# Attention, Fourier mixing and routed experts on one core: logits moved forward in the group, attention banks merged, readers of banks ahead, longer pauses

## The chip, the core and the metric

The kernel runs on one core of a Trainium2 chip. The metric is the device time of one execution in microseconds, the median of three runs. The core's engines work side by side, each through a queue of its own: TensorE (PE) multiplies matrices, VectorE (DVE), ScalarE (ACT) and GpSimd (POOL) work on elements, and the sync engine (SP) issues nearly all DMA transfers. TensorE writes its results to PSUM, eight banks of 2 KB in each of 128 partitions (512 numbers of 32 bits); another engine reads a bank before TensorE may fill it anew.

## What is computed

Three parts follow each other for 8 batches of 576 tokens of width 512: an attention through 32 packed queries, a mixing with a Fourier transform and a two-layer network, and a layer of eight experts of which each token takes one.

```python
p_packed = sm_attn(p, k, v)                 # 8 heads, p: 32 x 64, k and v: 576 x 64
out = sm_attn(q, p_packed, p_packed)
...
X = np.fft.fft(np.fft.fft(x, axis=1), axis=2)
u = x + np.real(X)
un = (u - mu) / np.sqrt(var + 1e-06)
x = u + np.maximum(un @ w_ch1, 0.0) @ w_ch2
...
logits = np.einsum('bsd,de->bse', x, w_gate)
local_gate = sigmoid(x @ w_local)           # under 0.5: the best expert of this token; else that of the token before
h = np.maximum(x[b, s] @ w1[e], 0.0)
out[b, s] = p[e] * (h @ w2[e])              # p: softmax of the logits
```

## The kernel before

Most products run on numbers split into two 16-bit parts, high and low, in three passes (PASS). First attention(0) runs alone (the first 81.5 us of the profile). Then come ten groups: b0, b1, b2, R0, b3, b4, b5, b6, R1, b7. A group bN is the channel mix of batch N (class Mix): 16 steps mm1(f) of 12 matmuls 512 columns wide into a bank hp, and 16 steps mm2(f) of 12 such matmuls into four banks acc, mm2 two steps behind mm1 (LEAD), 384 matmuls in all. ScalarE and VectorE make ht from hp between the two. R0 and R1 are the same for rows left over from four batches, half as wide. In the profile's rows the mix of b4 has the names hp18 and acc18 to acc21. Behind the groups the expert stage runs, from 1045.6 us.

Beside the mix of batch N runs, as a generator, attention(N + 1): at each tick of the mix (32 a group) it goes on by ATT_RATE yields. So a yield with nothing in front of it is a pause, and the attention's instructions stand between those of the mix, in an order that a scheduler then settles by priority when the program is built; high_priority(offset) lets an instruction pass others by that much (SOON 200, URGENT 100). In the order of a group the steps of the attention are:

- scores: s1 from k and the packed queries p, in two halves; greatest and exps read the banks; turn makes ehl and transposes it by DMA to et. The load of v is issued behind the scores, since it takes k's buffer.
- pps: et times v (vhl, two parts of v); ppr, ptp and pth are the packed result, scaled, transposed and split. The load of q is issued when v has been split, since it takes v's buffer; qh is q split by ScalarE and GpSimd.
- scores2, greatest2, exps2, sums2, divide2: s2 from q and pth, three tiles of 128, 128 and 99 rows; m2 and ee are read from its bank.
- channels: gp, the packed result times cosines and sines (cdt), four tiles of 257 columns (two halves, cosines and sines); g is gp split. fold2 and parts2 make eo, ah (transposed by DMA) and eh.
- bp (eh times cst), zd, then for three row tiles t: P and Q (cosine and sine part of the transform), qs a copy of Q, ul and uu (rl and ru for the leftover rows) sums and differences of P and qs, X (the attention's output itself), which is added to them. norm makes unh, transposed by DMA to ut, the input of the next group's mix.

After the mix of a batch, after_mix(tiles) runs as another generator at LAST_RATE yields a tick, beside the next group's mix: for each of the four tiles it scales u to xh, transposes it by DMA to xt (one buffer), stores it to XS, and multiplies it with the gate weights: lp, eight small matmuls, read by lsum. Expert weights are converted all the while (se, so, WS).

The eight PSUM banks are four for acc (psO), two for hp (psM), and two (psA) for all tiles of the attention and the logits: s1, pps, ptp, s2, gp, bp, zd, P, Q, X, lp.

## Time and profile before

| | before |
|---|---|
| median of 3 runs | 1516.62 us (1511.03 to 1521.59) |
| the profiled execution | 1514.66 us, span 1512.9 us from first to last instruction |
| TensorE busy | 1403.3 us, 93% of the span |
| VectorE, ScalarE, GpSimd busy | 769.0, 460.5, 278.9 us |
| mean granted clock of TensorE | 0.971 of full speed |

Busy time is a mean over stages of different kinds: it is to be read group by group, and where an engine stands idle the waits say which instruction of which other engine ended that. Granted clock is the share of full speed that the chip lets TensorE have; it has two levels, 1.2 and 2.4 GHz, and the value of a stretch is a mean of the two.

### The profile page before, as it was taken

The page shows a single profiled execution, that of the slowest core. Times are in us where ns is not written, and L with a number is a line of the kernel's source. Part 1 is how long each engine was busy: PE and PEld are TensorE (multiplying, and loading weights), DVE is VectorE, ACT ScalarE, POOL GpSimd, SP SyncE. Part 2 cuts the span into 40 slices and gives each one's busy share as a digit, 9 for nine tenths or more (in the row PEclk, how much of TensorE's full clock was granted, in tenths as well). Part 3 has the DMA queues.
Part 4 walks back from the last instruction along what each step waited for, and adds up shares of the span by engine and source line. Part 5 has one row for each costly group of instructions (what it writes and reads, how often), then busy time and mean ns, then how long its engine had stood idle before and what let it go on. Part 6 is the DMA issues. An engine that isn't in the chain of part 4 may idle for free. (4 is left out here: it accounts for less than half of the span.)

```text
span 1512.9 us, 28826 instructions
## 1 busy us (share of the span) xinstructions
PE 1403.3 (93%) x11340; PEld 825.5 (55%) x11340; DVE 769.0 (51%) x1615; ACT 460.5 (30%) x858; POOL 278.9 (18%) x296
## 2 busy tenths in 40 slices
PE   4588888998999899999999999999899999999996
PEld 3334434544564454454444456455677677777764
DVE  5789977567655766666766665433531111111110
ACT  3343444344333434434435333111111111111111
POOL 1312113203200420320321220000212121121211
PEclk6689999999999999999999999999999999999998
DMA  8275476386476637647656546244946636783371
GB/s 268 61 226 177 142 190 156 111 208 164 122 166 158 191 108 201 170 118 219 149 131 198 125 124 170 56 180 139 252 114 197 170 89 172 226 245 81 79 230 54
DMA packets 233163, 239.70 MB, mean 158 GB/s; under 512 B 168191, under 2 KB 179583, under 8 KB 232384
## 3 DMA queue, kind: packets, MB, share of 16 engines
q1 hardware_dynamic: 226464, 217.62, 52.6%
q0 software_dynamic: 6560, 20.19, 4.1%
q8 instruction: 91, 1.49, 0.4%
q14 instruction: 48, 0.39, 0.1%
HBM read 267.38 MB, written 53.74 MB: 212 GB/s over the span
## 5 line engine op out<-in xcount | busy, mean ns | idle before, releaser
L759 PE MATMUL acc<-w2h,ht 128*128 128x512 f16 x1728 | 410.3, 379 | 0.8 <-DVE ul L767 0.8
L739 PE MATMUL hp<-ut,w1h 128*128 128x512 f16 x1536 | 371.3, 383 | 5.9 <-DMA ut<-unh 5.2
L739 PEld LDWEIGHTS <-w1h 128*128 128x128 f16 x1920 | 183.7, 98 | 187.8 <-issue 21.0
L759 PEld LDWEIGHTS <-ht 128*128 128x128 f16 x1728 | 165.7, 98 | 185.2 <-issue 6.6
L1107 PE MATMUL ehp<-xgt,w1b 128*128 128x128 f16 x3936 | 232.6, 219 | 3.3 <-DMA w1b<-WS 2.2
L1107 PEld LDWEIGHTS <-w1b 128*128 128x128 f16 x3936 | 225.2, 98 | 15.5 <-DMA w1b<-WS 2.6
L1115 DVE SCALAR_TENSOR_TENSOR hx<-ehp,hx 128x512 f16<-128x512 f32 x82 | 56.6, 691 | 339.3 <-ACT hx L1114 335.5
L1125 PE MATMUL eo<-w2b,hx 128*128 128x512 f16 x984 | 219.2, 379 | 0.0
L747 DVE SCALAR_TENSOR_TENSOR ht<-hp,ht 128x512 f16<-128x512 f32 (+1 forms) x160 | 101.3, 633 | 165.9 <-ACT ht L746 165.7
L1125 PEld LDWEIGHTS <-hx 128*128 128x128 f16 x984 | 94.3, 98 | 106.3
L261 ACT ACTIVATE so<-se 128x512 f16<-128x512 f32 x128 | 79.8, 628 | 194.6 <-DMA WS<-so 154.6
L746 ACT ACTIVATE ht<-hp 128x512 f16<-128x512 f32 (+1 forms) x160 | 87.2, 546 | 138.6 <-PE hp L739 133.5
L1114 ACT ACTIVATE hx<-ehp 128x512 f16<-128x512 f32 x82 | 48.9, 597 | 185.9 <-PE ehp L1107 185.9
L262 DVE SCALAR_TENSOR_TENSOR so<-se,so 128x512 f16<-128x512 f32 x128 | 98.2, 776 | 10.7 <-ACT so L261 10.7
L1133 POOL DMA_INDIRECT out<-ys,sidx x41 | 41.5, 1013 | 332.2 <-ACT ys L1132 310.8
L1132 ACT ACTIVATE ys<-eo,scl 128x512 f32<-128x512 f32 x41 | 28.2, 687 | 179.2 <-PE eo L1125 179.2
L344 POOL TENSOR_TENSOR qh<-q,qh 128x1420 f16<-128x1420 f32 x12 | 34.6, 2880 | 257.3 <-ACT qh L343 233.9
L1075 POOL DMA_INDIRECT xg<-XS,gidx x41 | 42.2, 1029 | 174.9 <-DVE sidx L1031 103.9
L368 PE MATMUL s<-k,p 64*32 64x288 f32 x256 | 24.3, 478 | 24.8 <-DVE ru L648 11.6
L739 PE MATMUL hp<-utr,w1h 128*128 128x256 f16 x384 | 47.1, 272 | 0.0
L563 PE MATMUL bp<-cst,eh 128*128 128x289 f16 (+1 forms) x192 | 33.5, 317 | 13.2 <-ACT eh L540 6.5
L694 POOL TENSOR_TENSOR unh<-un,unh 128x512 f16<-128x512 f32 x32 | 38.6, 1216 | 30.7 <-ACT unh L693 30.7
(288 smaller groups left out, 1346.4 us busy)
## 6 DMA issues: line engine op xcount, KB each, us to landing
w1b<-WS SPq DMA_DIRECT2D x156, 512.0 KB
w2b<-WS SPq DMA_DIRECT2D x156, 512.0 KB
se<-in_w SPq DMA_DIRECT2D x64, 512.0 KB
WS<-so SPq DMA_DIRECT2D x128, 256.0 KB
sw<-in_wc SPq DMA_DIRECT2D x32, 512.0 KB
q<-in_qd SPq DMA_DIRECT2D x16, 710.0 KB
v<-in_vd SPq DMA_DIRECT2D x16, 640.0 KB
k<-in_kd SPq DMA_DIRECT2D x16, 576.0 KB
```

The costliest lines, as they stand in the source:

```text
L261: nc.scalar.activation(dst_hi, src, AF.Copy, scale=scale)
L262: nc.vector.scalar_tensor_tensor(dst_lo, src, scale, dst_hi, ALU.mult, ALU.subtract)
L739: nc.tensor.matmul(hp[:, :ntok], w1h[:, f, c, x], ut[:, 4 * y + c, :ntok], start=n == 0, stop=n == 11)
L746: nc.scalar.activation(ht[:, 0, :ntok], hp[:, :ntok], AF.Relu)
L747: pace[0] = nc.vector.scalar_tensor_tensor(ht[:, 1, :ntok], hp[:, :ntok], 0.0, ht[:, 0, :ntok], ALU.max, ALU.subtract).ins
L759: nc.tensor.matmul(self.acc[j], ht[:, x, 128 * j:128 * j + 128], w2h[:, f, y], start=f == 0 and n == 0, stop=f == 15 and n == 2)
L1075: nc.gpsimd.indirect_dma_start(out=g_, out_offset=None, in_=XS[0:rows], in_offset=bass.IndirectOffsetOnAxis(ap=gidx[:, b:b + 1], axis=0), ...
L1107: nc.tensor.matmul(hp[:, cols], w1b[b % RB][:, 2 * c + fg, x, cols], xt[b][:, 4 * y + c], start=n == 0, stop=n == 11, skip_group_check=True)
L1114: nc.scalar.activation(ht[:, fg, 0], hp, AF.Relu)
L1115: nc.vector.scalar_tensor_tensor(ht[:, fg, 1], hp, 0.0, ht[:, fg, 0], ALU.max, ALU.subtract)
L1125: nc.tensor.matmul(op, h[:, f // 4, x, 128 * (f % 4):128 * (f % 4) + 128], w2b[b % RB][:, f, y], start=n == 0, stop=n == 23)
L1133: nc.gpsimd.indirect_dma_start(out=A["out"], out_offset=bass.IndirectOffsetOnAxis(ap=sidx[:, b:b + 1], axis=0), in_=ys, in_offset=None, bo ...
```

## The change

Logits: LAST_RATE goes from 1.2 to 3, so that after_mix is done in the first third of the next group. Banks: cosines and sines share a gp tile of 512 columns (two of the sine's columns are always zero and are left out), so channels is called twice instead of four times; Q stands behind P in one bank for t < 2, and 24 small memsets on GpSimd set the two missing columns of qs to zero. Readers: the ScalarE and VectorE operations that read a bank of psA get an offset of 100 (freeing). Scores: only seven of the eight matmuls of a half get the offset of 200, so that they follow the first, which stands where the program has it. Pauses: one more yield ahead of pps (twice), behind pth and in each of the row tiles t, three more behind channels; ATT_RATE goes from 2.3 to 2.6. fold2 makes eo ahead of ah.

```diff
-    cd = np.concatenate([np.cos(2 * np.pi * ((c * k2) % 512) / 512), np.sin(2 * np.pi * ((c * k2) % 512) / 512)], 1)
+    cd = np.concatenate([np.cos(2 * np.pi * ((c * k2) % 512) / 512),
+                         np.sin(2 * np.pi * ((c * k2[:, 1:256]) % 512) / 512)], 1)
...
-ATT_RATE = 2.3
+ATT_RATE = 2.6
...
-LAST_RATE = 1.2
+LAST_RATE = 3
...
+    def freeing():
+
+        return tc.high_priority(offset=URGENT)
...
+            for n in range(8):
+                i, p2, r = n // 4, n // 2 % 2, n % 2
+                d, row = slice(64 * r, 64 * r + 64), 64 * p2 + 32 * r
+                with tc.high_priority(offset=SOON if n else 0):
+                    nc.tensor.matmul(s1[hf][i][row:row + 32, :288], pt[d, 2 * hf + p2],
+                                     kts[hf][d, p2, 288 * i:288 * i + 288], start=True, stop=True)
...
-                with tc.high_priority(offset=SOON if fn in (scores, greatest, exps) else 0):
+                with tc.high_priority(offset=SOON if fn in (greatest, exps) else 0):
...
+            yield
             n = 0
             for t in range(5):
...
-        nc.scalar.copy(pth[:, 0], ptp[:, :256])
-        nc.vector.tensor_tensor(pth[:, 1], ptp[:, :256], pth[:, 0], op=ALU.subtract)
+        with freeing():
+            nc.scalar.copy(pth[:, 0], ptp[:, :256])
+            nc.vector.tensor_tensor(pth[:, 1], ptp[:, :256], pth[:, 0], op=ALU.subtract)
...
-        yield
-        yield
+        for _ in range(3):
+            yield
...
-        g = ap.tile([128, 2, 2, 2, 257], F16, tag="g", name=f"g{b}")
...
+        g = ap.tile([128, 2, 2, 512], F16, tag="g", name=f"g{b}")
+
+        def channels(hf):
+            gp = att(f"gp{b}_{hf}")
             for n, (x, y) in enumerate(PASS):
                 for p2 in range(2):
...
+                    nc.tensor.matmul(gp[64 * p2:64 * p2 + 64],
                                      pth[:, x, 128 * hf + 64 * p2:128 * hf + 64 * p2 + 64],
...
+                                     cdt[:, 2 * hf + p2, y], start=n == 0, stop=n == 2, skip_group_check=True)
+            with freeing():
+                nc.scalar.copy(g[:, hf, 0], gp)
+                nc.vector.scalar_tensor_tensor(g[:, hf, 1], gp, 1.0, g[:, hf, 0], ALU.mult, ALU.subtract)
...
-            nc.vector.tensor_reduce(m2[:, 0], s3, axis=AX.X, op=ALU.max)
...
+            with freeing():
+                nc.vector.tensor_reduce(m2[:, 0], s3, axis=AX.X, op=ALU.max)
+                nc.vector.tensor_tensor(efs[i].rearrange("p (g j) -> p g j", j=32), s3,
+                                        m2[:, 0].unsqueeze(2).to_broadcast([nr, 16, 32]), op=ALU.subtract)
...
-                      ((channels, 1), (parts2, 1), (divide2, 2)), ((fold2, 2),), ((channels, 2), (parts2, 2)), (),
-                      ((channels, 3),), ()):
+                      ((parts2, 1), (divide2, 2)), ((fold2, 2),), ((channels, 1), (parts2, 2)), (), (), (), (), ()):
...
             P = att(f"P{b}_{t}")
-            Q = att(f"Q{b}_{t}") if t < 2 else P
+            Q = P[RQ, 257:512] if t < 2 else P[RQ, 1:256]
+            qs = qs0 if t == 0 else ap.tile([128, 576], F32, tag="f32w", name=f"qs{b}_{t}", bufs=4)
+            nc.gpsimd.memset(qs[R, 0:257:256], 0.0)
...
-                nc.tensor.matmul(Q[RQ, :257], bt[:, hf, x, 1, s0:s0 + M], g[:, hf, y, 1], start=n == 0, stop=n == 5,
+                nc.tensor.matmul(Q, bt[:, hf, x, 1, s0:s0 + M], g[:, hf, y, 257:], start=t == 2 and n == 0, stop=n == 5,
...
+            with freeing():
+                nc.scalar.copy(qs[R, 1:256], Q)
...
+            with freeing():
+                nc.vector.tensor_tensor(ul[R, :256], P[R, :256], qs[R, :256], op=ALU.subtract)
+                nc.vector.tensor_tensor(uu[R, :256], P[R, :256], qs[R, :256], op=ALU.add)
...
+            with freeing():
+                nc.vector.tensor_reduce(lsum, lp[:, :18].rearrange("p (y e) -> p e y", y=2), axis=AX.X, op=ALU.add)
```

Left out are the same wrappings around the operations that read bp, zd, X and the second half of P.

The built program shows what this moves. First TensorE in b4's group (names as above; lp12 to lp15 are the logits of b3's four tiles, and 5 is the attention of batch 5), before:

```order
L427 MATMUL pps5_6004<-vhl5_0_6005,et5_0_5949 64x128
...
L776 MATMUL lp12_6132<-wgh_110,xt12_5975 128x18
...
L442 MATMUL ptp5_6177<-ident_78,ppr5_6161 128x128 x2
...
L491 MATMUL s2_5_0_6215<-pth5_6194,qh5_0_6086 128x64
...
L776 MATMUL lp13_6301<-wgh_110,xt13_6158 128x18
...
L491 MATMUL s2_5_2_6313<-pth5_6194,qh5_0_6086 128x64
...
L469 MATMUL gp5_0_6370<-cdt_94,pth5_6194 64x257
...
L469 MATMUL gp5_1_6420<-cdt_94,pth5_6194 64x257
...
L469 MATMUL gp5_2_6464<-cdt_94,pth5_6194 64x257
...
L469 MATMUL gp5_3_6489<-cdt_94,pth5_6194 64x257
...
L776 MATMUL lp14_6510<-wgh_110,xt14_6367 128x18
...
L563 MATMUL bp5_0_0_6529<-cst_92,eh5_0_6400 128x289
```

And TensorE in the same group, after:

```order
L373 MATMUL s1_5_0_0_5801<-k5_0_5797,p5_5794 32x288 x2
...
L373 MATMUL s1_5_1_0_5845<-k5_1_5799,p5_5794 32x288 x2
...
L793 MATMUL lp12_5897<-wgh_110,xt12_5825 128x18
...
L793 MATMUL lp13_5964<-wgh_110,xt13_5918 128x18
...
L433 MATMUL pps5_5928<-vhl5_0_5929,et5_0_5874 64x128
...
L793 MATMUL lp14_6054<-wgh_110,xt14_6017 128x18
...
L793 MATMUL lp15_6146<-wgh_110,xt15_6073 128x18
...
L497 MATMUL s2_5_0_6189<-pth5_6158,qh5_0_6039 128x64
...
L497 MATMUL s2_5_2_6261<-pth5_6158,qh5_0_6039 128x64
...
L476 MATMUL gp5_0_6319<-cdt_94,pth5_6158 64x512
...
L476 MATMUL gp5_1_6394<-cdt_94,pth5_6158 64x512
...
L569 MATMUL bp5_0_0_6444<-cst_92,eh5_0_6346 128x289
```

Counted in matmuls of the mix from the group's start, the scores s1_5 stood 24 and 13 ahead of the start, at the end of b3's group, and stand at 54 and 65 now; pps at 96 and 117, now 97 and 120; the logits at 120, 171, 219 and 279, now 80, 97, 117 and 141; the last s2 at 171, now 168; the four gp at 180, 189, 201 and 210, now two at 180 and 198; the first bp at 222, now 225. P and Q of t = 0 stood at 249 and the second X behind them at 270, both unchanged. Groups b2, b3, b5 and b6 look alike, but in b3 the scores stood at 36 to 56 before already, with pps at 84 and s2 at 141.

The sync engine's queue in the same stretch, before (v, q and k are loads from memory, WS1, WS2 and XS stores, se loads of expert weights):

```order
L329 DMA v5_0_5892<-in_vd 128x5x256
L329 DMA v5_1_5937<-in_vd 128x5x256
L391 DMA_TRANSPOSE et5_0_5949<-ehl5_0_5945 128x10x128
...
L334 DMA q5_0_6015<-in_qd 128x1420
L391 DMA_TRANSPOSE et5_1_5982<-ehl5_1_5978 128x10x128
...
L334 DMA q5_1_6078<-in_qd 128x1420
L798 DMA_TRANSPOSE xt12_5975<-xh12_5942 128x8x128
L799 DMA XS_124<-xh12_5942 128x1024
...
L798 DMA_TRANSPOSE xt13_6158<-xh13_6058 128x8x128
```

And the sync engine's queue there, after:

```order
L334 DMA v5_0_5811<-in_vd 128x5x256
L816 DMA_TRANSPOSE xt12_5825<-xh12_5816 128x8x128
...
L334 DMA v5_1_5855<-in_vd 128x5x256
...
L396 DMA_TRANSPOSE et5_0_5874<-ehl5_0_5870 128x10x128
L816 DMA_TRANSPOSE xt13_5918<-xh13_5867 128x8x128
...
L396 DMA_TRANSPOSE et5_1_5913<-ehl5_1_5909 128x10x128
L339 DMA q5_0_5949<-in_qd 128x1420
...
L816 DMA_TRANSPOSE xt14_6017<-xh14_5954 128x8x128
...
L339 DMA q5_1_6028<-in_qd 128x1420
L816 DMA_TRANSPOSE xt15_6073<-xh15_6036 128x8x128
```

The loads of q5 were issued 9 and 38 matmuls into the group and are issued at 97 and 112 now; v5 and the transposes et5, ahead of or at the group's start before, now stand among four transposes for logits (xt12 at 65, xt13 at 85, xt14 at 104, xt15 at 120).

VectorE around the last s2 of that group, before (m2 and ee read its bank, g reads gp's):

```order
L498 TENSOR_REDUCE m2_5_2_6354<-s2_5_2_6313 99x16
L526 SCALAR_TENSOR_TENSOR ah5_0_6379<-ee5_0_6280,ah5_0_6379 128x512
L500 TENSOR_TENSOR ee5_2_6356<-s2_5_2_6313,m2_5_2_6354 99x512
L530 SCALAR_TENSOR_TENSOR eo5_0_6383<-ee5_0_6280 128x256
L518 TENSOR_TENSOR ee5_1_6292<-ee5_1_6292,m2_5_1_6290 128x512
L747 SCALAR_TENSOR_TENSOR ht18_7_6364<-hp18_7_6297,ht18_7_6364 128x512
L474 SCALAR_TENSOR_TENSOR g5_6214<-gp5_0_6370,g5_6214 128x257
```

And VectorE there, after:

```order
L506 TENSOR_REDUCE m2_5_2_6306<-s2_5_2_6261 99x16
L522 TENSOR_REDUCE m2_5_1_6254<-t16_5_1_6303 128x16
L507 TENSOR_TENSOR ee5_2_6307<-s2_5_2_6261,m2_5_2_6306 99x512
L532 SCALAR_TENSOR_TENSOR eo5_0_6328<-ee5_0_6243 128x256
L540 SCALAR_TENSOR_TENSOR ah5_0_6331<-ee5_0_6243,ah5_0_6331 128x512
L523 TENSOR_SCALAR m2_5_1_6254<-m2_5_1_6254 128x16
L524 RECIPROCAL m2_5_1_6254<-m2_5_1_6254 128x16
L525 TENSOR_TENSOR ee5_1_6255<-ee5_1_6255,m2_5_1_6254 128x512
L764 SCALAR_TENSOR_TENSOR ht18_7_6316<-hp18_7_6290,ht18_7_6316 128x512
L481 SCALAR_TENSOR_TENSOR g5_6188<-gp5_0_6319,g5_6188 128x512
```

Between the first reader of the last s2 and the second stood ah, and stands a small reduction now; ee5_2 gives the bank free, and g5 the bank of gp5_0.

## Rows read from the trace of the kernel before

**Rows 1.** Busy us by stretch (first stretch, b0's group, b4's), clock, DMA share, GB/s.

```profile
0.00:81.50 81.50, 39.62 (x289) 28.00 (x290) 52.92 (x112) 25.79 (x57) 22.59 (x44) 0.67 0.53 161
...
81.50:198.50 117.00, 107.13 (x641) 53.13 (x641) 105.92 (x207) 47.22 (x90) 19.81 (x22) 0.98 0.60 180
...
581.10:690.70 109.60, 105.31 (x713) 52.26 (x712) 72.15 (x148) 45.26 (x86) 24.90 (x24) 0.98 0.61 167
```

**Rows 2.** TensorE's waits: who waited for whom, total us, times, longest us.

```profile
PE s L368 <- DVE ru L648: 11.6, 2, 9.5
...
PE lp L776 <- DVE g L474: 8.0, 5, 2.0
...
PE s L368 <- issue: 7.1, 3, 2.6
...
PE gp L469 <- DVE ee L500: 4.6, 3, 2.3
...
PE bp L563 <- DVE g L474: 4.3, 5, 1.2
...
PE gp L469 <- DVE g L474: 3.9, 4, 1.2
...
PE gp L469 <- DVE lsum L780: 2.0, 2, 1.1
```

**Rows 3.** Timeline at the end of b3's group: start, duration in us, [idle before <- releaser].

```profile
571.28 0.40 DVE L648 TENSOR_TENSOR ru<-P,qs 32x256 f32<-32x256 f32 x1
...
571.78 0.69 PE L368 MATMUL s<-k,p 64*32 64x288 f32 x8 [2.58 <-issue]
```

**Rows 4.** Busy us in steps of 3 us at two places; granted clock third from last.

```profile
371.00:374.00 3.00, 1.85 (x13) 0.73 (x13) 3.00 (x7) 1.06 (x3) 0.00 (x0) 0.64 0.11 22
...
374.00:377.00 3.00, 3.00 (x16) 1.73 (x15) 1.11 (x4) 1.26 (x3) 0.00 (x0) 0.80 0.85 244
...
860.00:863.00 3.00, 3.00 (x10) 1.17 (x9) 0.66 (x2) 1.56 (x3) 0.00 (x0) 0.50 1.01 251
...
863.00:866.00 3.00, 3.00 (x21) 1.95 (x20) 1.33 (x3) 1.29 (x3) 0.00 (x0) 0.95 0.52 160
```

**Rows 5.** Timeline in b4's group, the logits between gp and bp.

```profile
636.58 0.67 DVE L526 SCALAR_TENSOR_TENSOR ah<-ee,ah 32x512 f16<-32x512 f32 x1
...
637.18 0.41 DVE L474 SCALAR_TENSOR_TENSOR g<-gp,g 128x257 f16<-128x257 f32 x1
...
637.64 0.17 PE L776 MATMUL lp<-wgh,xt 128*128 128x18 f16 x1 [2.01 <-DVE g L474]
```

**Rows 6.** Timeline in b3's group, from the load of q to s2.

```profile
487.32 0.43 SPq L334 DMA_DIRECT2D q<-in_qd  x1
...
487.35 1.03 PE L427 MATMUL pps<-vhl,et 128*64 128x128 f16 x30 [0.91 <-DMA et<-ehl]
...
488.31 2.76 PE L739 MATMUL hp<-ut,w1h 128*128 128x512 f16 x12
...
490.91 2.11 PE L759 MATMUL acc<-w2h,ht 128*128 128x512 f16 x9
...
493.23 1.38 ACT L343 CAST qh<-q 128x1420 f16<-128x1420 f32 x1 [1.52 <-DMA q<-in_qd]
...
504.92 0.21 PE L491 MATMUL s<-pth,qh 128*128 128x64 f16 x1 [2.64 <-ACT pth L448]
```

**Rows 7.** Timeline in b7's group: a transpose for logits and the logits.

```profile
965.45 1.24 SPq L798 DMA_TRANSPOSE xt<-xh  x1
...
968.60 0.18 PE L776 MATMUL lp<-wgh,xt 128*128 128x18 f16 x1 [0.75 <-DMA xt<-xh]
```

**Rows 8.** Groups by line: busy us, mean ns of one, idle before them.

```profile
L344 POOL TENSOR_TENSOR qh<-q,qh 128x1420 f16<-128x1420 f32 x12 | 34.6, 2880 | 257.3 <-ACT qh L343 233.9 <-PE acc L759 23.4
...
L469 PE MATMUL gp<-cdt,pth 128*64 128x257 f16 x192 | 17.1, 293 | 10.7 <-DVE ee L500 4.6 <-DVE g L474 3.9 <-DVE lsum L780 2.0
...
L474 DVE SCALAR_TENSOR_TENSOR g<-gp,g 128x257 f16<-128x257 f32 x32 | 13.1, 410 | 0.5 <-ACT g L473 0.5
```

More of the change, by code (lines that the diff above doesn't have):

```diff
@@ L124, in prep @@
     k2 = np.arange(257)[None, :]
[L125 removed]
+    cd = np.concatenate([np.cos(2 * np.pi * ((c * k2) % 512) / 512),
+                         np.sin(2 * np.pi * ((c * k2[:, 1:256]) % 512) / 512)], 1)
     cd = np.stack(split(cd), 1)
[L127 removed]
+    o["cdt"] = np.ascontiguousarray(cd.reshape(4, 128, 2, 512).transpose(1, 0, 2, 3))
     pp = np.arange(128)
@@ L362, in scores @@
             s1[hf] = [att(f"s1_{b}_{hf}_{i}") for i in range(2)]
-            for i in range(2):
-                for p2 in range(2):
-                    for r in range(2):
-                        d, row = slice(64 * r, 64 * r + 64), 64 * p2 + 32 * r
-                        nc.tensor.matmul(s1[hf][i][row:row + 32, :288], pt[d, 2 * hf + p2],
-                                         kts[hf][d, p2, 288 * i:288 * i + 288], start=True, stop=True)
+            for n in range(8):
[4 more added lines that the diff above has]
+                                     kts[hf][d, p2, 288 * i:288 * i + 288], start=True, stop=True)
             (load_v if b else load_q)(hf)
@@ L522, in fold2 @@
             na = min(nr, 288 - 128 * i)
-            ah = ap.tile([128, 2, 640], F16, tag="h16", name=f"ah{b}_{i}", bufs=5)[:na].rearrange(
-                "p a n -> p (a n)")[:, :1024]
-            nc.scalar.activation(ah[:, :512], ef[:na], AF.Copy, scale=2.0 ** -4)
-            nc.vector.scalar_tensor_tensor(ah[:, 512:], ef[:na], 2.0 ** -4, ah[:, :512], ALU.mult, ALU.subtract)
-            nc.sync.dma_start_transpose(out=at[:, :, 128 * i:128 * i + na], in_=ah)
             eo = eos[i] = ap.tile([128, 576], F32, tag="f32w", name=f"eo{b}_{i}", bufs=4)[:nr, :512]
@@ L534, in fold2 @@
             nc.gpsimd.tensor_tensor(eo[:, 256:], ef[:, :256], ef[:, 256:], op=ALU.subtract)
+            ah = ap.tile([128, 2, 640], F16, tag="h16", name=f"ah{b}_{i}", bufs=5)[:na].rearrange(
+                "p a n -> p (a n)")[:, :1024]
+            nc.scalar.activation(ah[:, :512], ef[:na], AF.Copy, scale=2.0 ** -4)
+            nc.vector.scalar_tensor_tensor(ah[:, 512:], ef[:na], 2.0 ** -4, ah[:, :512], ALU.mult, ALU.subtract)
+            nc.sync.dma_start_transpose(out=at[:, :, 128 * i:128 * i + na], in_=ah)
         def parts2(i):
@@ L577, in attention @@
                     for (x, y) in PASS:
-                        nc.tensor.matmul(zd[:, :257], zt[:, hf, x], g[:, hf, y, 0], start=n == 0, stop=n == 5)
+                        nc.tensor.matmul(zd[:, :257], zt[:, hf, x], g[:, hf, y, :257], start=n == 0, stop=n == 5)
                         n += 1
-                nc.scalar.copy(qs0[:64, 288:545], zd[:64, :257])
+                with freeing():
+                    nc.scalar.copy(qs0[:64, 288:545], zd[:64, :257])
                 yield
@@ L604, in p_mm @@
                 hf, x, y = terms[n]
-                nc.tensor.matmul(P[R, :257], bt[:, hf, x, 0, s0:s0 + M], g[:, hf, y, 0], start=n == 0, stop=n == 5,
+                nc.tensor.matmul(P[R, :257], bt[:, hf, x, 0, s0:s0 + M], g[:, hf, y, :257], start=n == 0, stop=n == 5,
                                  skip_group_check=True)
@@ L630, in attention @@
             yield
-            qs = qs0 if t == 0 else ap.tile([128, 576], F32, tag="f32w", name=f"qs{b}_{t}", bufs=4)
-            nc.scalar.copy(qs[R, :257], Q[RQ, :257])
+            with freeing():
+                nc.scalar.copy(qs[R, 1:256], Q)
             if t == 0:
@@ L657, in attention @@
                         x_mm(X, R, lu, n)
-                nc.vector.tensor_tensor(ut[R], ut[R], X[(RL, RU)[lu]], op=ALU.add)
+                with freeing():
+                    nc.vector.tensor_tensor(ut[R], ut[R], X[(RL, RU)[lu]], op=ALU.add)
                 yield
@@ L779, in logits @@
             lsum = wp.tile([128, 9], F32, tag="lsum", name=f"lsum{col}", bufs=2)
-            nc.vector.tensor_reduce(lsum, lp[:, :18].rearrange("p (y e) -> p e y", y=2), axis=AX.X, op=ALU.add)
+            with freeing():
+                nc.vector.tensor_reduce(lsum, lp[:, :18].rearrange("p (y e) -> p e y", y=2), axis=AX.X, op=ALU.add)
             nc.vector.tensor_scalar(LG[:, col], lsum, RSC[:, col:col + 1], 2.0 ** -20, ALU.mult, ALU.mult)
```

37 lines of the change are left out of this document (14 added, 23 removed).

## The prediction

> **What bounds the kernel now.** I read the busy time by stretch first. In the seven groups in which matmuls of the channel mix alternate with the attention of the next batch, TensorE is busy 105.31 of 109.60 us in b4's group [rows 1]; in b0's it is 107.13 of 117.00, and there VectorE is busy 105.92 of 117.00, so b0 has two engines at their limit [rows 1]. The first 81.5 us hold only 39.62 us of TensorE work [rows 1], but they are a chain of small steps that this change hardly touches. The expert stage behind 1045.6 us is not touched. What the change can win is therefore TensorE's idle time inside the seven groups, and what that idle time does to its clock.
>
> Next the list of TensorE's waits [rows 2]. The reader is to see that the waits which are not in the first stretch are nearly all for a PSUM bank: logits wait for g, the reader of a gp bank, 8.0 us in five waits; gp waits for the readers ee (4.6), g (3.9) and lsum (2.0); bp waits for g (4.3). Together that is 22.8 us. The attention draws from two banks, and each waiting matmul holds up all of the mix behind it, because TensorE takes its queue in order.
>
> The third view is the boundary between groups. The scores of the next batch stand at the end of the old group and wait for the four U operations that read the bank of P: the last of them starts at 571.28, and the scores start at 571.78 after 2.58 us of idle time [rows 3]. The list puts three of these under "issue" (7.1 us) and one under ru (11.6 less the longest, 9.5, which lies in the first stretch, leaves 2.1) [rows 2].
>
> The fourth view is the granted clock. After the logits' wait near 371 us three microseconds ran at 0.64 and the next three at 0.80; after the one near 860 at 0.50 and 0.95 [rows 4]. At half speed work takes double, so a dip costs (1 - 0.64) x 3 + (1 - 0.80) x 3 = 1.7 us, and the other one 1.65. In these groups there are five such dips, all behind waits of about 2 us; these two are the first and the last.
>
> **The change part by part.** *Scores behind the two leading steps.* In the steady groups they now stand 54 matmuls into the next group, when the U operations have long read their bank. The waits of 7.1 and 2.1 go: 9.2 us.
>
> *Banks merged, logits moved away from them, readers first.* Two gp tiles instead of four, the second one 18 matmuls behind the first instead of 9, no logits between them, and bp 27 matmuls behind the last gp. A 512-wide matmul of the mix takes 0.217 us at full clock ((2.76 - 2.11) / 3) [rows 6], so these distances are 3.9 and 5.9 us. A reader pair is one ScalarE copy and one VectorE operation; VectorE's part takes 0.41 us for 257 columns [rows 8] and, twice as wide, some 0.8 (an estimate from it). Before, g stood in VectorE's queue behind ah, which nobody on TensorE was waiting for: ah at 636.58, g at 637.18, then the logits at 637.64 after 2.01 us [rows 5]. Readers first takes that away too. Of the 22.8 us I leave out one group of seven, 3.3, since b0's VectorE has no room, and 1.5 more for waits that stay: 18 us. The bounds are 12 and 21.
>
> *The clock.* Three of the five dips follow the logits' waits, one the scores', one the s2 matmuls'. Four of them go: 4 x 1.7 = 6.7 us (bounds 3 and 8.4).
>
> *Longer pauses and pth first.* In b3's group s2 waited 2.64 us for pth [rows 6]; with pth's copies ahead and a third pause I count 2.0 of it (bounds 0 and 4, the pauses before pps and zd included).
>
> *Fewer, wider gp matmuls.* 192 matmuls are busy 17.1 us, 0.089 us each [rows 8]. 96 of double width at double cost would save nothing; at no more than the start-up that is saved, 2 us. I take 1. The 24 small memsets on GpSimd, the reordering of eo and ah and the changes in the first stretch I cost at nothing: they lie beside chains of several us; if GpSimd were late with a memset it would delay a qs copy, which has 21 matmuls before its bank is wanted. Q's two missing columns and the zeros in qs change nothing that counts.
>
> *What the change adds.* The scores move later, and their followers move with them: the v load waits for the scores (it takes k's buffer), the q load for v. In b4's group q5_1 stood 38 matmuls into the group and is now at 112, with s2 at 156; the logits' transposes now stand among these loads on the sync queue. The trace has a model for it, b3's group, whose scores came late already (42 matmuls before pps, now 43). There pps waited 0.91 us [rows 6]. A q load took from 487.32 to 493.23, 5.9 us, then the cast 1.38 [rows 6] and GpSimd's subtraction 2.88 [rows 8]: 10.2 us. Between q5_1 and s2 lie 44 x 0.217 = 9.5 us and a pps set of 1.03 [rows 6], 10.6 in all; that just covers it, and I count 0.6 us of wait (bounds 0 and 2.64, b3's wait). A transpose for logits lands 3.15 us after issue where nothing delays it (965.45 to 968.60) [rows 7]; from xt13 to its logits there are now 12 matmuls, 2.6 us: a wait of 0.55. Sum 0.91 + 0.6 + 0.55 = 2.1 us in each of the four groups that have this new (b2, b4, b5, b6), 8.2 us, 0.55 in b1 makes 9, and two new clock dips, 3.4: 12.4 us lost. Bounds: 2 if all lands in time, 4 x (0.91 + 2.64 + 1.1 + 2 x 1.7) = 32 if nothing does.
>
> The Trainium skill speaks against this part: "DMA: Bandwidth & Descriptors", section "Rules for kernel authors", advises to issue a transfer early, compute, and wait late. This change issues v and q later and waits as soon as before. By that rule alone the four groups would pay the upper bound, and the sum would stand near 1511. The trace agrees as far as it goes: of the groups b3 to b6 it is the late one, b3's, whose matmuls wait at pps and at s2.
>
> **The sum.** 9.2 + 18 + 6.7 + 2.0 + 1 = 36.9 us won, 12.4 lost: 24.5 us. The profiled execution took 1514.66 us (1.8 beyond its span), 2 us under the median of the three runs, 1516.62, well inside their spread. So 1490 by the one and 1492 by the other; I say 1491.
>
> **The rivals.** *The waits move on instead of going.* TensorE, freed of one wait, comes sooner to the next reader, and VectorE's and ScalarE's queues set the pace. For it: b0, where VectorE is busy nine tenths. Against it: in b4's group VectorE has a third of its time free (72.15 of 109.60) [rows 1]. Then only the boundary waits, half of the bank waits and two dips are won, 9.2 + 9 + 3.4, and 12.4 are lost: 1507. With the upper bound of the loss nothing is won.
>
> *The loads come too late: slower.* ScalarE takes its queue in order too: while it stands at the cast for q it can't make ht, and the second matmul of the mix wants ht 24 matmuls (5.2 us) later. It stood there 1.52 us in b3's group [rows 6]. If the load of q, now issued in a heap with v, two logits transposes and their stores, took over 5.9 + 5.2 = 11 us, TensorE would stand still for the mix itself. Two such stops of 4 us and two dips in each of four groups cost 4 x (8 + 3.4) = 46 us more: 1537. Against it: no load of that kind in the trace took so long.
>
> *Everything goes.* If the waits vanish and the loads land in time, 46 us are won and 4 lost: 1475.
>
> That the change does not do what it says is excluded by the order of the built program: scores, logits, gp and bp stand where I said.
>
> **How the numbers follow.** Forecast, 1481 to 1501: 0.53. Everything goes, 1467 to 1480: 0.16. Waits move on, 1502 to 1530: 0.23. Too late, over 1531: 0.08. A difference under 1%, 15 us, can't be told from none here. So faster by over 1% (under 1501.5) has 0.69, within 1% 0.23, slower 0.08. The range leaves out the slow case and the ends of the two others: 1467 to 1520.
>
> **What would show it.** In the profile after: no waits of lp or bp for g, and those of gp down to 1 to 3 us; no wait of the scores in b2 to b6; new waits of pps for et, s2 for qh, lp for xt, together some 9 us; fewer stretches under full clock between 300 and 900 us; the groups b4 to b6 shorter by 2 to 4 us each, b1 by 6, b0 hardly. The prediction would be wrong if ScalarE's idle time before qh grew past 5 us, if TensorE waited for ht, or if the first stretch moved by more than 2 us.

## The result, and the profile after

The changed kernel took 1522.16 us (median of 20 runs, 1518.96 to 1528.54), the kernel before 1513.76 us in the same comparison (20 runs, 1504.92 to 1521.59): a ratio of 1.0056, 95% interval 1.0041 to 1.0072. So the change made the kernel slower by 8 us, where 1491 us and a gain were forecast; 1522 lies above the range too.

First the busy time by stretch of the changed kernel: the first stretch, b0's group and b4's, the columns as in [rows 1].

```profile
0.00:80.70 80.70, 39.12 (x276) 26.04 (x277) 54.43 (x108) 25.39 (x51) 21.98 (x47) 0.64 0.54 161
80.70:199.75 119.05, 111.76 (x645) 55.34 (x645) 109.34 (x210) 46.81 (x88) 19.49 (x25) 0.97 0.60 177
573.54:686.11 112.57, 106.60 (x702) 53.25 (x701) 70.84 (x144) 44.62 (x83) 24.15 (x27) 0.97 0.60 162
```

The first stretch is the same within a microsecond. b4's group was to be 2 to 4 us shorter and is 3.0 us longer than in [rows 1], at 0.97 of the clock in place of 0.98. From the first matmul of b1's group to the end of R1's, the attention groups of the two kernels lasted

```profile
198.50:952.18 753.68, 715.82 (x4868) 371.71 (x4869) 485.33 (x991) 295.18 (x563) 152.75 (x148) 0.99 0.59 158
```

before, and after

```profile
199.75:961.73 761.98, 715.53 (x4796) 371.97 (x4797) 471.63 (x982) 292.53 (x553) 149.75 (x166) 0.98 0.58 157
```

which is 8.3 us more: as much as the whole difference. TensorE stood idle for 37.9 us of the stretch before and for 46.5 after. (At its first edge 16 matmuls of b0's mix, some 3.5 us, stand inside it before and ahead of it after, so on equal work the groups grew by some 12 us and what comes ahead of them shrank by some 2.) The groups don't move together: b1's is 10.6 us shorter (3.5 of them by that edge) and b3's 6.5, while b2, b4, b5 and b6 are 5.9, 3.0, 2.9 and 5.1 longer, R0 2.5 and R1 6.1. Shorter b1 was forecast; R0 and R1 had no term in the sum.

TensorE's waits in the changed kernel, as in [rows 2]:

```profile
PE lp L793 <- DMA xt<-xh: 25.6, 15, 4.4
...
PE bp L571 <- DVE eh L551: 11.3, 6, 2.9
PE s L373 <- DVE rl L675: 11.0, 1, 11.0
PE bp L569 <- DVE big L574: 8.6, 5, 2.5
...
PE s L373 <- issue: 2.1, 1, 2.1
```

The waits of lp and bp for g and all of gp's, 22.8 us in [rows 2], are gone, and so are the scores' at the groups' ends (what is left of them lies in the first stretch). In their place logits wait for their transposed tokens, 25.6 us in 15 waits (4.0 us in 4 before), and bp waits for eh (11.3) and for big (8.6), the reader of the bank of the bp ahead of it; before, these were 1.2 and 0.3 us. In the groups b1 to R1 alone 18.6 us of the 22.8 went, and 20.2 us for xt and 18.8 for eh and big came. Where the logits stand in b4's group, TensorE and then SyncE's queue (start, duration, [idle before <- releaser]):

```profile
600.30 0.20 PE L793 MATMUL lp<-wgh,xt 128*128 128x18 f16 x1 [2.73 <-DMA xt<-xh]
```

```profile
592.50 1.94 SPq L396 DMA_TRANSPOSE et<-ehl  x1
594.54 2.21 SPq L816 DMA_TRANSPOSE xt<-xh  x1
596.85 0.54 SPq L314 DMA_DIRECT2D WS<-so  x1
597.52 2.21 SPq L396 DMA_TRANSPOSE et<-ehl  x1
599.78 0.58 SPq L339 DMA_DIRECT2D q<-in_qd  x1
```

xt was issued at 594.54, straight behind a transpose of the attention, and the logits could start at 600.30: 5.8 us, where [rows 7] showed 3.15. And the clock behind that wait, with its second step to be set beside [rows 4] (granted clock third from last):

```profile
597.00:600.00 3.00, 0.58 (x3) 0.08 (x1) 0.66 (x3) 0.72 (x1) 0.00 (x0) 1.00 1.27 161
600.00:603.00 3.00, 2.69 (x40) 2.14 (x41) 1.16 (x6) 1.75 (x4) 0.00 (x0) 0.52 1.16 238
603.00:606.00 3.00, 3.00 (x14) 1.27 (x13) 2.15 (x2) 1.95 (x3) 0.00 (x0) 0.91 1.19 294
```

That dip cost (1 - 0.52) x 3 + (1 - 0.91) x 3 = 1.7 us. Summed over all steps of 3 us between 81 and 1071 us, the lost clock came to 10.6 us before and 18.8 after, in one execution of each.

### The profile page after: what moved, and what is told of

The parts are those of the page before. It is cut to its first block, busy times and chain, and to the rows that moved or that the text cites. A ratio compares the mean times of both kernels' runs of the same rounds, so it can differ in the third digit from the quotient of the medians.

```text
span 1520.4 us, 28635 instructions
## 1 busy us (share of the span) xinstructions
PE 1405.1 (92%) x11244; PEld 824.7 (54%) x11244; DVE 759.5 (50%) x1599; ACT 457.1 (30%) x842; POOL 279.6 (18%) x320
## 5 line engine op out<-in xcount | busy, mean ns | idle before, releaser
L776 PEld LDWEIGHTS <-ht 128*128 128x128 f16 x1728 | 167.2, 99 | 189.5 <-issue 10.6
L1093 POOL DMA_INDIRECT xg<-XS,gidx x41 | 46.6, 1136 | 180.5 <-DVE sidx L1049 110.6
```

The lines of the kernel that those rows point to most:

```text
L776: nc.tensor.matmul(self.acc[j], ht[:, x, 128 * j:128 * j + 128], w2h[:, f, y], start=f == 0 and n == 0, stop=f == 15 and n == 2)
L1093: nc.gpsimd.indirect_dma_start(out=g_, out_offset=None, in_=XS[0:rows], in_offset=bass.IndirectOffsetOnAxis(ap=gidx[:, b:b + 1], axis=0), ...
```

## The experiments

Two theories stood at first. **A**: the logits, placed in the first third, cost what the rest of the change gained. **B**: the bank part gained nothing, since each wait only moved on to the next bank. Ratios are to the kernel before, run beside each kernel on the same chip.

**Logits back.** `e1_logits_back`: the changed kernel with

```
-LAST_RATE = 3
+LAST_RATE = 1.2
```

> The changed kernel with its logits put back to the later places that they had (the rate of their spreading again 1.2, all else as changed). Theory A, that the logits placed early cost what the rest of the change gained: TensorE's waits of logits for the transposed tokens xt fall from 25.6 us to about 4, most of the half-clock stretches that stand behind them go too (some 6 us), so about 1522 - 21 - 6 + 4 (waits of logits for banks that come back in part, of 8.0 before) = about 1499 us, at most 1508. Theory B, that the merged banks gained nothing because each wait only moved to the next bank: the waits of logits for xt turn into waits for other things and the time stays within 1516 to 1525 us.

Ratio 0.9961 (0.9937 to 0.9984), 1509.14 us: 14 us faster than the changed kernel by the two ratios, and a little faster than the kernel before. The waits for xt fell to 6.7 us as theory A has it, but it came out 10 us short of A's 1499. For the rest other waits came up, as theory B has it; that the merged banks gained nothing doesn't follow, and e12 below shows otherwise.

```profile
PE gp L476 <- DVE lsum L798: 10.2, 5, 3.5
PE bp L569 <- DVE big L574: 7.5, 6, 3.0
PE s L497 <- DVE pth L456: 5.6, 6, 1.5
```

bp's waits for eh fell from 11.3 to 4.5 us as well, so most of their growth came with the early logits. (This profile is of the longest of the kernel's 12 runs, 1515.59 us.)

**Logits forward alone.** `e2_logits_forward`: the kernel before with `LAST_RATE = 3`.

> The kernel before with one part of the change alone: logits in the first third of the next group (rate 3 in place of 1.2). Theory A: the waits for xt come up here as well, some 4 us to 18 us more than before's 4.0, against 8.0 us of logits waiting for the bank under g that go; with the half-clock stretches the kernel is slower than before by 5 to 15 us (1519 to 1529 us). Theory B: the logits' place is nearly free, within 5 us of before (1509 to 1519 us).

Ratio 1.0049 (1.0024 to 1.0074): slower by 7.4 us, with 18.9 us of waits for xt; the logits' 8.0 us of waits for g went. Theory A holds in the kernel before as well. The room is short here even for a transpose that nothing delays: in seven of the 13 waits for xt of the groups b1 to R1 (15.7 us in all) the logits started 3.1 to 3.5 us after the issue, close to the 3.15 of [rows 7], and each of the seven was issued as soon as its tokens xh were made. The longest of them, in R1:

```profile
923.25 0.75 DVE L791 SCALAR_TENSOR_TENSOR xh<-ul,rsc,xh 128x512 f16<-128x512 f32 x1 [0.54 <-ACT xh L790]
924.03 1.23 SPq L798 DMA_TRANSPOSE xt<-xh  x1
927.14 0.18 PE L776 MATMUL lp<-wgh,xt 128*128 128x18 f16 x1 [2.87 <-DMA xt<-xh]
```

**A second buffer for xt.** `e3_two_xt_buffers`: the changed kernel with

```
-            xt = wp.tile([128, 8, 128], F16, tag="xt", name=f"xt{col}", bufs=1)
+            xt = wp.tile([128, 8, 128], F16, tag="xt", name=f"xt{col}", bufs=2)
```

> The changed kernel with two buffers for the transposed tokens in place of one, so that a group's second transpose doesn't wait until the first logits have read theirs (room for it: the third pass's t16 shares a buffer with ppr, and the gate's one-hot has one buffer in place of two). Theory A1, that the single buffer makes the transposes late: logits' waits for xt fall from 25.6 us to under 8, time about 1500 to 1508 us. Theory A2, that the transposes are late because they queue behind the loads of v and q and the transposes of e on the same queue: waits for xt stay above 18 us and the time above 1515 us.

Ratio 1.0026 (1.0005 to 1.0047). The waits for xt were still 22.4 us, as theory A2 had it: the single buffer is not what makes most of the transposes late. Whether it costs a few us can't be told; this interval and the changed kernel's overlap.

**A rate between.** `e4_logits_between`: the changed kernel with `LAST_RATE = 2`.

> The changed kernel with the logits' rate 2 in place of 3: they then lie at 90, 120, 150 and 186 of a group's matrix products, in place of 79, 96, 117 and 141. Theory A: room of 30 products (some 7 us) between two logits covers the transposes, which took 3.8 to 6.8 us from issue to logits: waits for xt under 8 us, time about 1500 to 1508 us. Theory B (waits only move): 1516 to 1525 us.

Ratio 0.9989 (0.9968 to 1.001), 1512.08 us, between the runs at 3 and at 1.2, as are its 15.5 us of waits for xt. More room means less waiting; 7 us of it didn't yet cover the transposes, so the expected "under 8" was missed.

**What holds the banks' readers up.** In the run with the logits back I followed the longest waits to their start. First TensorE, VectorE and ScalarE around a gp that waited 3.54 us for lsum, the reader of the logits' bank (timeline):

```profile
735.14 1.28 PE L476 MATMUL gp<-cdt,pth 128*64 128x512 f16 x6 [3.54 <-DVE lsum L798]
```

```profile
732.70 0.29 DVE L522 TENSOR_REDUCE m<-t 128x16 f32<-128x128 f32 x1 [5.02 <-POOL t L517]
...
734.93 0.16 DVE L798 TENSOR_REDUCE lsum<-lp 128x9 f32<-128x18 f32 x1
```

```profile
727.31 0.63 ACT L266 ACTIVATE so<-se 128x512 f16<-128x512 f32 x1 [3.91 <-DMA WS<-so]
730.11 0.63 ACT L266 ACTIVATE so<-se 128x512 f16<-128x512 f32 x1 [2.17 <-DMA WS<-so]
730.65 1.13 ACT L511 ACTIVATE ee<-ee 128x512 f32<-128x512 f32 x2
```

The logits had been done since 729.6. lsum stood in VectorE's queue behind m, which waited 5.02 us for GpSimd's t; that waited for the exponentials ee; and those stood in ScalarE's queue behind two splits of expert weights, which waited for the stores of their buffers, 3.91 and 2.17 us. A bp that waited 3.01 us for big lay behind ScalarE directly:

```profile
753.75 0.63 ACT L266 ACTIVATE so<-se 128x512 f16<-128x512 f32 x1 [5.86 <-DMA WS<-so]
754.28 0.40 ACT L573 ACTIVATE big<-bp 128x289 f16<-128x289 f32 x1
```

In the changed kernel three of the four waits of bp for big over 1.5 us in the groups read like this one, and in the kernel before so do the four waits of the scores at the ends of groups, that of [rows 3] among them: ahead of ru a copy qs stands on ScalarE behind a split that had waited 2.02 us for its store. That gave **theory C**: the readers are late because a split that waits for its DMA stands ahead of them, and not, **theory D**, because there are too few banks.

**A third buffer for the split.** `e5_logits_back_so3` (on the run with the logits back) and `e6_before_so3` (on the kernel before):

```
-                    so = wp.tile([128, 2, 512], F16, tag="so", name=f"so{e}_{k}_{a}", bufs=2)
+                    so = wp.tile([128, 2, 512], F16, tag="so", name=f"so{e}_{k}_{a}", bufs=3)
...
-            t16 = ap.tile([128, 16, 16], F32, tag="t16", name=f"t16_{b}_{i}")[:nrs[i]]
+            t16 = ap.tile([128, 16, 16], F32, tag="pp1", name=f"t16_{b}_{i}")[:nrs[i]]
```

> The changed kernel with its logits back at their later places (as in the run before with rate 1.2, 1509 us) and with three buffers so for the split expert weights in place of two (room: the third pass's t16 shares a buffer with ppr, the gate's one-hot has one buffer). Theory C, that the banks' readers are late because ScalarE and VectorE take their work in order and a split so<-se that waits for its buffer's store to DRAM (WS<-so) stands ahead of them: waits of bp for big (7.5 us), of gp for lsum (10.2) and part of those of s for ee (4.0) go, some 15 us in all, ScalarE's idle time for WS<-so (177 us) falls by more than half, time 1490 to 1500 us. Theory D, that the readers are late because VectorE is busy (the banks are too few whatever ScalarE does): the waits stay and the time stays within 1505 to 1512 us.

> The kernel before with the same third buffer so (and the same room made for it), nothing else. Theory C: some of the waits of the next batch's first scores at a group's end (7.1 us put down to issue, 2.1 to ru) and of zd (2.5) lie behind a split that waits for its store, those of bp, lp and gp for g don't (VectorE is busy ahead of them); so 5 to 9 us go, 1507 to 1511 us against 1516. Theory D: within 3 us of before.

Ratios 1.002 (1.0002 to 1.0039) and 1.0127 (1.0106 to 1.0148): both slower than the kernel each was made from, which neither theory had. ScalarE's waits of the first of the two:

```profile
ACT so L266 <- DMA se<-in_w: 124.5, 52, 7.6
ACT so L266 <- DMA WS<-so: 110.2, 41, 5.3
```

In the run with two buffers these waits were 177.3 us for WS and 3.5 for se. With a third buffer the split stands at the same place and waits for the load of the next weights as well, so the experiment didn't take the wait away, and the waits of gp (11.2 us) and bp (6.7) stayed. Why the time grew by 9 us in the one and by 19 in the other (by the ratios) is not settled. The buffer that t16 shares came in with it, but e3 has that too and was not slower than the kernel that it was made from.

**The splits out of the groups.** `e11_no_splits_in_groups`, the run with the logits back, and `e13_change_no_splits`, the changed kernel, each with `EW_RATE = 0`, so that all splits are made in one piece at the end of the last attention part. They show the groups only; the whole takes 1680 and 1694 us.

> The changed kernel with its logits back (1509 us; in its profile the groups from b1 to R1 lasted 751.7 us and TensorE waited 44 us in them), with the splitting of the expert weights taken out of the groups and done in one piece at the end of the last attention part, where it costs far more (100 us or more, which is not the question). What is read is the groups alone. Theory C, that readers of banks stand behind splits that wait for their DMAs: waits of bp for big and of gp for lsum (17.7 us there) all but vanish, and the groups last 15 to 30 us less. Theory D, that the banks are short whatever the splits do: these waits stay over 10 us, and the groups last no more than 8 us less.

The groups b1 to R1 with the splits (first), and without them (second):

```profile
201.65:953.39 751.74, 708.69 (x4780) 369.53 (x4781) 477.13 (x978) 290.87 (x553) 154.39 (x166) 0.99 0.59 159
```

```profile
200.66:908.83 708.17, 699.73 (x4781) 369.48 (x4782) 388.18 (x851) 224.70 (x427) 145.69 (x166) 1.00 0.32 76
```

43.6 us less, more than the 15 to 30 expected; TensorE's waits make 35 of them (43.1 to 8.4 us of time not busy). Of the waits that are left there, the longest and gp's for lsum:

```profile
PE pps L433 <- DMA et<-ehl: 4.1, 3, 1.5
PE pps L433 <- DVE vhl L421: 2.3, 1, 2.3
...
PE gp L476 <- DVE lsum L798: 1.1, 5, 0.2
```

gp's wait for lsum fell from 10.2 to 1.1 us and bp's for big from 7.5 to nothing, with the same banks in the same order. That decides against theory D: the banks suffice when the splits are away. It isn't yet proof of theory C, since the splits' work and traffic left together with their waits (DMA share 0.59 to 0.32); that the waits are what blocks the readers rests on the timelines above.

> The changed kernel whole (logits early), with the splitting of the expert weights taken out of the groups and done in one piece at the end of the last attention part, where it costs 100 us or more, which is not the question. What is read are the logits' waits for xt in the groups (up to the end of R1: some 20 of the 25.6 us). Theory A2, that the transposes come late because SyncE's queue, ScalarE and VectorE are full of the splits and their loads and stores: those waits fall under 5 us. Theory A3, that the time from a transpose's issue to its data, and the work on the tokens ahead of it, is simply longer than the room that rate 3 leaves: they stay over 12 us.

TensorE's waits of 2 us or more in all, in the groups of that run:

```profile
PE lp L793 <- DMA xt<-xh: 17.3, 10, 4.1
PE pps L433 <- DMA et<-ehl: 2.2, 1, 2.2
```

In the same stretch the changed kernel has 20.2 us in 12 waits for xt. Without the splits nearly everything else is gone and these are still there: theory A3. The groups b1 to R1 of this run,

```profile
197.46:922.33 724.87, 705.37 (x4797) 369.78 (x4797) 390.44 (x855) 225.48 (x427) 144.07 (x166) 0.99 0.32 75
```

last 16.7 us longer than those of e11, from which it differs in the rate of the logits alone. What stands ahead of an xt in SyncE's queue is now the attention's own first third:

```profile
569.99 3.27 SPq L396 DMA_TRANSPOSE et<-ehl  x1
573.36 2.25 SPq L816 DMA_TRANSPOSE xt<-xh  x1
575.71 2.60 SPq L396 DMA_TRANSPOSE et<-ehl  x1
578.36 0.58 SPq L339 DMA_DIRECT2D q<-in_qd  x1
579.55 1.23 SPq L816 DMA_TRANSPOSE xt<-xh  x1
```

The logits behind the xt of 573.36 started at 579.17, after 4.11 us of idle time: 5.8 us again. In the queue this xt took 2.25 us behind an et, and the one of 579.55, not directly behind one, 1.23.

Read one by one, the 12 waits for xt of the changed kernel's groups are of three kinds, but for one of 0.2 us. In six of them (12.2 us) the xt was issued within 0.2 us behind the issue of an et, 2.3 to 2.9 us after its tokens were made, and the logits started 3.4 to 6.6 us after that. In three (3.5 us) it was issued 0.4 us after the logits ahead of it had started, the readers of its only buffer. In two, the first of R0 and of R1 (4.4 us), it was issued as soon as its tokens were made, and took 3.1 and 3.9 us. No run moved the transposes et away, so the part of the queue is read from traces and not tried.

**Scores late alone.** `e7_scores_late`: the kernel before with

```
+            for n in range(8):
+                i, p2, r = n // 4, n // 2 % 2, n % 2
...
+                with tc.high_priority(offset=SOON if n else 0):
...
-                with tc.high_priority(offset=SOON if fn in (scores, greatest, exps) else 0):
+                with tc.high_priority(offset=SOON if fn in (greatest, exps) else 0):
```

> The kernel before with one part of the change alone: of a group's eight score products seven come forward and the first keeps its later place, so that all eight come behind the leading steps of the next group. The prediction's term: 9.2 us of waits at the groups' ends go, time about 1507 us. Rival: the scores' softmax, which then starts later, moves the wait to pps and ptp in the next group, and the time stays within 4 us of before (1512 to 1520 us).

Ratio 1.0023 (1.0004 to 1.0042): no gain, rather a small loss. TensorE's waits:

```profile
PE s L491 <- DVE pth L449: 10.0, 6, 3.0
PE s L368 <- DVE ru L648: 9.3, 1, 9.3
```

The scores' waits in the groups are gone (the 9.3 is the first stretch's), and s2 waits for the two halves of pth 10.0 and 1.4 us, against 0.2 and 2.6 before: 9.4 us gone, 8.6 come. The rival of that expectation had it right, one step later than it said.

**Readers first taken off.** `e8_no_readers_first`: the run with the logits back, with `freeing()` giving no priority.

> The changed kernel with its logits back at their later places (1509 us), and without the early places of the banks' readers (the priority of 100 taken off everywhere that the change gave it). If readers first is worth what the prediction made of it (part of its 18 us), the waits for g, big and ee grow by 5 to 12 us: 1514 to 1521 us. If readers first only moves other work (splits, ht) behind and gains nothing: 1506 to 1512 us.

Ratio 0.9943 (0.9921 to 0.9966), against 0.9961 with it: no gain from readers first; whether it costs 3 us or nothing can't be told, the intervals overlap.

**Merged banks with pauses, and alone.** `e9_banks_pauses_only` is that run with the scores put back too, `e12_banks_only` the same with the pauses and the rate of the attention part of before:

```
-ATT_RATE = 2.6
+ATT_RATE = 2.3
...
-        for _ in range(3):
+        for _ in range(2):
...
-    ((parts2, 1), (divide2, 2)), ((fold2, 2),), ((channels, 1), (parts2, 2)), (), (), (), (), ()):
+    ((parts2, 1), (divide2, 2)), ((fold2, 2),), ((channels, 1), (parts2, 2)), (), (), ()):
```

> What is left of the change when logits, scores and the readers' priority are put back as they were: the merged banks, the longer pauses, the order in fold2. If the parts add up: the run without readers first stood 8.6 us under before (ratio 0.9943), and the scores' move cost 3.4 us when made alone (1.0023), so about 12 us under before, some 1500 us. If they don't add (the late scores covered something that the merged banks need): no better than the run without readers first, 1503 to 1512 us.

> The run of merged banks and pauses alone (e9) with the pauses and the attention rate of before (2.3, one empty step less ahead of the fifth product block, two fewer behind the parts, one less in each third): merged banks alone. The prediction put 2 us on the pauses and most of 18 us on the banks. If the banks carry it: within 3 us of e9. If the pauses carry it: 5 to 12 us slower than e9, as before or slower.

Ratios 0.9916 (0.9883 to 0.9949) and 0.9919 (0.9887 to 0.995): 1501.74 and 1501.25 us, faster than both kernels. The parts add up, what e12 keeps (the merged banks and the order in fold2) carries the gain, and the pauses carry nothing. But the gain isn't seen where the prediction sought it. TensorE's waits in e12:

```profile
PE s L373 <- issue: 9.4, 4, 2.7
PE bp L568 <- DVE g L480: 7.8, 3, 2.7
...
PE gp L475 <- DVE ee L506: 0.7, 1, 0.7
```

lp no longer waits for g, and gp's waits for banks are down to 1.1 us; bp's for g grew from 4.3 to 7.8. In the groups b1 to R1 lp, gp and bp together waited 18.8 us before and 15.7 in e12, and TensorE's idle time there is 34.7 us against 37.9 (in e9 it is 38.1):

```profile
198.80:943.22 744.42, 709.71 (x4788) 367.64 (x4789) 478.64 (x978) 293.84 (x553) 152.36 (x166) 0.99 0.59 160
```

So most of the waits moved on to bp, and where the 12 us of the ratio lie isn't shown. One profile of each can't tell: even the expert stage, which no edit touches, is 4.9 us shorter in e12's than in before's.

**Where splits and stores could go.** `e10_stores_on_gpsimd` is e9 with the stores on another queue; `e14_banks_only_splits_longer` is e12 with the splits spread into b7's group:

```
-                    nc.sync.dma_start((WS1 if k < 4 else WS2)[e, :, c0:c0 + 1024], so.rearrange("p x n -> p (x n)"))
+                    nc.gpsimd.dma_start((WS1 if k < 4 else WS2)[e, :, c0:c0 + 1024], so.rearrange("p x n -> p (x n)"))
```

```
-EW_RATE = 1.3
+EW_RATE = 1.1
...
         if early:
+            drain(ew)
             for b in range(2):
                 load_w1(b)
...
-                drain(ew)
                 drain(last)
```

> The kernel of merged banks and pauses alone (e9), with the stores of the split weights (WS<-so) issued by GpSimd in place of SyncE. Theory C1, that the splits wait because their stores and loads stand in SyncE's queue behind transposes of 1 to 3 us each: ScalarE's waits of so for WS fall well under 160 us, TensorE's waits fall by 5 us or more, and the time is 5 to 10 us under e9. Theory C2, that GpSimd, which then waits in order for VectorE's part of each split, delays sums and eh: the waits of m for t and of bp for eh grow and the time is 3 to 15 us over e9.

> Merged banks alone (1501 us) with the splits spread thinner, rate 1.1 in place of 1.3; what is left of them (some 15%) runs on into the last group, which has no attention part, up to the first load of an expert's weights. Taking all splits out of the groups b1 to R1 shortened them by 43 us; 15% of the splits thus are worth about 6 us if the cost goes by their number, and the last group has room for them: 1493 to 1498 us. Rival: the first expert's weights then come late (their load waits for the last store), and the experts start late: 1501 to 1515 us.

Stores on GpSimd: 1.0583 (1.0546 to 1.062), far beyond what theory C2 feared. ScalarE's wait for these stores grew to 290.8 us (148.5 in e9), and TensorE waited 14 to 20 us in each of the groups b1 to b6. GpSimd's issues of the stores waited 146.8 us in 39 waits for VectorE's part of the split, and they stand in its queue ahead of sums and eh.

The Trainium skill, "DMA: Bandwidth & Descriptors", section "Rules for kernel authors", says that spreading DMAs over issuing engines doesn't help bandwidth and saves sequencer time only. This run agrees that nothing is won, and shows a loss beside it.

The splits spread longer: 0.9931 (0.9906 to 0.9956), no better than e12. The groups b1 to R1 lasted 743.5 us (744.4 in e12), so some 15% fewer splits gave next to nothing there, and b7's group took 9.5 us more, at 0.93 of the clock:

```profile
940.86:1043.84 102.98, 99.25 (x494) 48.52 (x493) 46.33 (x127) 23.11 (x40) 4.21 (x4) 0.93 0.59 192
```

against 93.43 us at full clock in e12. This profiled execution took 1508.52 us, 6 over the median of its kernel, so the 9.5 may be too much; that the cost of the splits goes by their number is not borne out.

## Why the prediction was wrong, step by step

Put in a row, each kernel with one part of the change more than the one above it (neighbouring intervals overlap but for the last step, so the ends and that step are what is clear):

| kernel | ratio | 95% interval |
|---|---|---|
| merged banks, order in fold2 (e12) | 0.9919 | 0.9887 to 0.9950 |
| and longer pauses (e9) | 0.9916 | 0.9883 to 0.9949 |
| and scores late (e8) | 0.9943 | 0.9921 to 0.9966 |
| and readers first (e1) | 0.9961 | 0.9937 to 0.9984 |
| and logits at rate 2 (e4) | 0.9989 | 0.9968 to 1.0010 |
| and logits at rate 3: the change | 1.0056 | 1.0041 to 1.0072 |

1. **The loss, and in it the logits: the step that failed first.** The term was "from xt13 to its logits there are now 12 matmuls, 2.6 us: a wait of 0.55", with 3.15 us "where nothing delays it". It took one transpose of a group for all, put its issue where it stands in the program's order, and took a latency from a place where the queue is empty. I made it 0.55 us in each of five groups, 2.75 in all; the groups showed 20.2 us, and 17.3 with the splits away. The transposes were issued late, behind the attention's et, behind the logits that still read their buffer, or because their tokens were only just made, and behind an et they took up to 6.6 us. R0 and R1, where early logits waited 5.4 us, were left out. At close to 3.15 us the room was short as well, as e2 shows for the kernel before. In time the logits' move costs 14 us in the changed kernel (0.9961 to 1.0056), 7.4 us alone, and 16.7 us of the groups without the splits, in place of a gain counted within the 18 us.
2. **The loads of q and v, the loss's other part,** came out smaller than forecast: pps waited 0.22 us in b3's group where [rows 6] had 0.91, and no s2 waited for a late q. 1.51 us in each of four groups was counted. So the change came out slower by another mechanism than the rival "the loads come too late" named (no matmul waited for an ht behind a qh).

   The rule of the Trainium skill that the prediction weighed ("DMA: Bandwidth & Descriptors", "Rules for kernel authors": issue early, wait late) was read onto v and q alone; it bears as much on xt, whose room between issue and use shrank. The measurement agrees with it there: 20.2 us of waits.
3. **Scores, 9.2 us:** the waits went exactly as counted and came back as waits of s2 for pth: nothing gained (e7). What would be late next was asked of the loads only, not of the softmax behind the scores.
4. **Banks, 18 us:** right in direction, too large, and the mechanism only half borne out. In the changed kernel lp, gp and bp wait no longer for g, and by its ratio e12 is worth 0.8%, 12 us, an interval of 8 to 17. But the waits did not go as counted: in e12 most of them moved on to bp. Readers first, counted in the 18, gave nothing. The timelines show readers late because their engine stands at a split, and being ahead of ah or ht doesn't help there. What a reader overtakes can itself be wanted soon, though whether that costs anything isn't shown (bp's waits for eh are 4.5 us with readers first in e1 and 5.5 without in e8). In b4's group of the changed kernel g runs between the two halves of eo, and bp waits 2.91 us for eh, which needs eo:

```profile
636.85 0.97 DVE L534 SCALAR_TENSOR_TENSOR eo<-ee,c 99x256 f32<-99x256 f32 x1
637.74 0.68 DVE L481 SCALAR_TENSOR_TENSOR g<-gp,g 128x512 f16<-128x512 f32 x1
638.35 0.34 DVE L535 TENSOR_SCALAR eo<-eo,c 99x256 f32<-99x256 f32 x1
```

5. **Clock, 6.7 us won, two dips lost:** the gain didn't come; in the two profiled executions some 8 us more were lost than before. That the new waits cost this much clock isn't shown: e2, with 18.9 us of the same waits, lost 9.3 in its profile, less than before's 10.6, and the changed kernel's runs have a mean clock of 0.962 to 0.980, those of the kernel before beside e1 0.963 to 0.985.
6. **Pauses, 2 us:** nothing (e9 against e12). **Wider gp, 1 us:** right in direction; 96 matmuls were busy 14.5 us in place of 192 for 17.1 [rows 8], so 2.6. The term was set between nothing and 2 us with no row behind the 2.

The rival "the waits move on instead of going" was the one that held, for the scores, for the readers and for most of the banks' waits, and 1522 lies in its interval, which had 0.23. Its own sum of 1507 is near what the change does without the logits' move (e1, 1509), but by luck in part: it counts the boundary waits as won, which came back, and a loss that was mis-sized. What stays open: where the merged banks' 12 us lie, and how much of the splits' 43 us is their waiting, how much their work and their traffic.

## What to carry to other kernels

A latency read where a queue is empty came out as about the least that the same transfer takes elsewhere: before work is moved up, count what the queue holds at the new place, take the latency of the same transfer beside such neighbours, and ask when the transfer can be issued at all: its data must be made and its buffer read. And before a wait for a buffer is answered with more buffers, wider spacing or priority, follow its reader back along its own engine's queue: here the engine stood at an unrelated instruction that waited for a DMA, and waits that were removed at one place (the scores', lp's and gp's) were found again one step further on.

## What the runs showed of the hardware that was not expected

Background work on engines that were not the bound cost TensorE much time: without the splits ScalarE was busy 66 us less and VectorE 89 us less in the groups (of 291 and 477 in 752 us), and the groups lost 43.6 us, while TensorE's clock in them went from 0.99 to 1.00. In the changed kernel's groups a DMA transpose xt issued directly behind another transpose took up to 3.1 us in the queue, against a median of 1.27 of all, and up to 6.6 us from its issue to the matmul that used it, against 3.15 in [rows 7]. And stores of 256 KB issued by GpSimd in place of SyncE made the kernel 5.8% slower than the one before (its neighbour e9 is 0.8% faster than that one), though GpSimd was busy only a quarter of the time in the groups (223 of 848 us).
